# Opening of a convolution and SwiGLU kernel: how block 0's x is cut and loaded, when the first weights and block 1's x are issued, and one tap of the opening's plan

## The chip, the cores and the metric

The kernel runs on one core of one Trainium2 chip. The metric is the device time of one execution in microseconds (us). Three executions before the change took 771.68 (the median), 770.90 and 772.23 us. Times within the kernel are counted from the start of the profiled span.

The engines are named as in the profile: PE is TensorE's matmul, PEld its weight load, DVE is VectorE, ACT is ScalarE, POOL is GpSimd, SP is SyncE, which here only issues DMAs and passes semaphores on. A small q (SPq, POOLq) marks an engine's sequencer. Lines as L553 are lines of the kernel before the change.

## The reference: what is computed

A causal convolution of seven taps along the sequence, with softmaxed weights per head, and behind it a SwiGLU block. There are 8 sequences of 4096 tokens with 192 channels, 8 heads of 24 channels, and 1536 channels inside the second part.

```python
w = np.exp(weight - weight.max(-1, keepdims=True))
w = w / (w.sum(-1, keepdims=True) + 1e-09)                  # 8 heads x 7 taps
x_pad = concatenate([zeros((B, 6, D)), x], axis=1)          # causal
idx = arange(S)[:, None] + arange(7)[None, :]
out = einsum('hk,bskhg->bshg', w, x_pad[:, idx, :].reshape(B, S, 7, 8, 24))
x = out.reshape(32768, 192)
g = x @ w_gate
y = (g * (1 / (1 + exp(-g))) * (x @ w_val)) @ w_out         # 192 -> 1536 -> 192
```

## The kernel before

**Blocks and chunks.** The 32768 tokens are 64 blocks of 512, taken in 32 pairs. In a block the 1536 inner channels are 12 chunks of 128. For one chunk TensorE makes `gate` (L546) and `val` (L547) from the convolved x, three steps of 64 rows each, both at a time on the two halves of the array; ACT takes silu of the gate (L551), DVE multiplies it with val into `h` (L553), and TensorE multiplies h by `wo_sb` into `acc` (L558), one block behind. Chunks are counted through the whole kernel: 0 to 11 are block 0, 12 to 23 block 1, and so on. `late_start` gives the units of L558 in chunks 12 to 19: none in 12 and 13, six each from 14 on. After twelve units, at the end of chunk 15, the accumulation changes halves, and the next L558 has to wait for the last of the first half. That is done through `mark` (L440): a no-operation on SP that waits for the matmul, and for which the later matmul waits.

**Two ways to convolve.** From the second pair on, the convolution is done on channels by partitions: x is loaded in 32 x 32 squares (`emit_load`, L103, tiles sqA, sqB, and headA, headB for a sequence's first pair), transposed on DVE (`emit_turn`, L114, tiles xtA, xtB), and the seven taps are shared out by a plan: tap 0 on ACT into a PSUM bank, `run` (L473), further taps on ACT (L466), DVE (L483) or POOL (L488), and POOL adds the products and makes `xc` (L495, L501). The products of ACT and POOL cost one addition on POOL each, apart from the first; DVE's are added as they are made. SP then swaps the halves of xc (L449, L450) into `xs`. Each pair has three such groups. `plan_group` puts each step behind a chunk; `PLAN["opening"]` gives them for pair 1, as (turn, start, taps on ACT, taps on DVE, POOL, join, swap), one row for each group.

The first pair is convolved on TensorE, so that it can start without the transposed x. x is loaded token by token on partitions, in six overlapping pieces (windows) of a block, 85 tokens apart (`load_x`, tile x_sb, fp32; index 0 is block 0 and 1 is block 1). Block 0's pieces 3 to 5 go from ACT's queue, 1 and 2, then 0, and then all of block 1's from SP's. The band matrix of the taps, T, is built meanwhile: softmax on DVE and ACT (`wmax`, `soft`, `spun`, `left`), L310 (`repeat`) on TensorE, and four products with the 0/1 matrix `band` on DVE (L318, `cut_band`). The copy `flat` (L376) is one of their inputs. ACT and POOL cast block 0's pieces to fp16 (L229, tile x16); `heads` multiplies them by T (L334), two per head group, and `gather` (L392) puts channels into the order of the second part: D0, D1, D2, the operands of block 0's gate and val. Block 1's pieces are cast by POOL into x16p (L232, two casts, by parity of the head), and `lateA(0)`, `lateA(1)` and `lateC` convolve them in chunks 2, 5 and 8, with 48 matmuls of L334 each, into `foldA1` and `foldC1`, whose halves SP swaps for block 1 (L661).

**The orders around the change.** Each engine's instructions run in the order of the program. POOL: the four iotas (L171), `plain` and `mask` (L201 to L211), weights 0 to 3 (two DMAs, `load_w`, L158; they cast from fp32 to fp16), its cast of block 0's x, `spread` places 0 and 1, weights 4 to 7, places 2 and 3, `own`, the two casts of x16p, weights 8 to 11, `wo`, and then group 1's taps. SP: taps, block 0's x, block 1's x, the four headB loads of pair 1 (shown as sqB; they wait for the first `repeat`, L364), the first halves of headA (behind `lateA(0)`, L655), the swaps of foldA1 and foldC1, the second halves of headA (chunk 9), the swap of group 1 (chunk 13), and pair 2's loads from chunk 14 on.

PSUM: gates of block 0 rotate through two banks; those of chunks in `PLAN["third"]` (2 and 10) take the `run` bank instead, which group 1's tap 0 uses in between.

Of the kernel before, what the change touches and what calls it, by code (L numbers as in the profile page):

```python
# [15 lines left out]
    load=((2, -47), (3, -40), (0, -34), (1, -28)),  # L16
    opening=(
# [3 lines left out]
    ),  # L21
    gate=2, val=3, lead=4, third=(2, 10),
)


# [1 line left out]
def kernel(  # L27
# [9 lines left out]
    nc = tc.nc  # L37
# [16 lines left out]
    NCH = Dff // P  # L54
    pad = K - 1
# [3 lines left out]
    n_pairs = NT // (2 * TB)  # L59
    ppb = S // (2 * TB)  # L60
    x_flat = x.flatten_outer_dims()
# [14 lines left out]
    squares, xts = {}, {}  # L76
# [5 lines left out]
    def emit_load(q, part, half=None):  # L82
        head = q % ppb == 0
        if part == 2 and not half:
            squares[q, "A"] = headA if head else xpool.tile(
                [P, HIST + 2 * TB], fp32, tag="sqA", name="sqA"
            )
            squares[q, "B"] = headB if head else xpool.tile(
                [P, HIST + TB], fp32, tag="sqB", name="sqB"
            )  # L90
        for k in range(2):
            quad = 2 * (part % 2) + k
            if part < 2:
                tile_, t0, n, c = squares[q, "A"], 0, 2 * TB, SQ * quad
            else:
                tile_, t0, n, c = squares[q, "B"], TB * (part % 2), TB, P + SQ * k
            skip = HIST if head and t0 == 0 else 0
            row = q * 2 * TB + t0 - HIST + skip
            n = n // SQ + 1 - skip // SQ
            if half is not None:  # L100
                first = TB // SQ + 1
                skip, row, n = ((skip, row, first), (first * SQ, row + first * SQ, n - first))[half]
            nc.sync.dma_start(  # L103
                out=tile_[quad * SQ : (quad + 1) * SQ, skip : skip + n * SQ].rearrange("p (n c) -> p n c", c=SQ),
                in_=x_flat[row : row + n * SQ, c : c + SQ].rearrange("(n p) c -> p n c", p=SQ),
            )
# [9 lines left out]
    def sync_after(ins, earlier, why="one bank, two halves of the array"):  # L116
        tc.add_manual_dep(
            ins.ins,
            earlier.ins.name,
            mybir.DependencyInfo(mybir.DependencyClass.Sync, mybir.DependencyReason.DATA),  # L120
            reason=why,
        )

    HALF, STEP, W, NW = TB // 2, 85, 88, 6
    ROWS, LOADED = W + pad, 96
    ends = (0, STEP, 2 * STEP, HALF, 4 * STEP, 5 * STEP, TB)
    assert 8 == K + 1 and (NW - 1) * STEP + W > TB and HALF - 3 * STEP in (0, 1)
    RT = 8 * H  # L130
    taps = const_pool.tile([H, K], fp32, tag="taps", name="taps")
    nc.sync.dma_start(out=taps, in_=weight)
    x_sb = xpool.tile([P, 2, NW, D], fp32, tag="x_sb", name="x_sb", bufs=1)

    def load_x(b, lo, hi, skip=0, queue=nc.sync):
        queue.dma_start(
            out=x_sb[skip:LOADED, b, lo:hi, :],
            in_=bass.AP(
                tensor=x_flat.tensor,
                offset=x_flat.offset + (b * TB + lo * STEP - pad + skip) * D,  # L140
                ap=[[D, LOADED - skip], [STEP * D, hi - lo], [1, D]],
            ),
        )

    load_x(0, 3, NW, 0, nc.scalar)
    load_x(0, 1, 3)
    load_x(0, 0, 1, pad)
    load_x(1, 0, NW)
    w = wpool.tile([P, 3, Dff], fp16, tag="w_sb", name="w_sb")
    wo_r = wpool.tile([P, NCH, D], fp16, tag="wo_sb", name="wo_sb")  # L150
    w_halves = [
# [4 lines left out]
    def load_w(lo, hi, which):  # L156
        rows, src = w_halves[which]
        nc.gpsimd.dma_start(out=w[rows, :, lo * P : hi * P], in_=src[:, :, lo * P : hi * P])  # L158
# [4 lines left out]
    nc.vector.memset(one, 1.0)  # L163
    two = const_pool.tile([P, 1], fp32, tag="two", name="two")
    nc.scalar.activation(two, one, AF.Exp)
    nc.vector.memset(x_sb[0:pad, 0, 0, :], 0.0)


    def numbers(name, shape, pattern, base, dt=int32, step=1):
        t = const_pool.tile(shape, dt, tag=name, name=name)  # L170
        nc.gpsimd.iota(  # L171
            t, pattern=pattern, base=base, channel_multiplier=step, allow_small_or_imprecise_dtypes=True
        )
        return t
# [1 line left out]
    head = numbers("head", [H, H, 8], [[-1, H], [0, 8]], 0)  # L176
    far = numbers("far", [RT, 8, K], [[-1, 8], [1, K]], 8)
    row = numbers("row", [RT, RT], [[-1, RT]], 0)
    off = numbers("off", [P, W], [[-1, W]], 0)

    whose = const_pool.tile([H, H, 8], fp32, tag="whose", name="whose")
    rotate = const_pool.tile([RT, 8, K], fp32, tag="rotate", name="rotate")
# [3 lines left out]
    def where(out, t, bits):  # L186
# [11 lines left out]

    plain = const_pool.tile([P, 4, grp], fp16, tag="plain", name="plain")
    spread = const_pool.tile([P, 4, 2, DB], fp16, tag="spread", name="spread")  # L200
    nc.gpsimd.memset(plain, 0.0)  # L201
    nc.gpsimd.affine_select(
        out=plain, in_=plain, pattern=[[-32, 4], [-1, grp]],
# [8 lines left out]
        out=mask[:, :].rearrange("r (h c) -> r h c", h=H),  # L212
# [1 line left out]
        pattern=[[-8, H], [0, grp]],  # L214
        compare_op=ALU.not_equal, fill=1.0, base=0, channel_multiplier=1,
    )
    load_w(0, 4, 0)
    load_w(0, 4, 1)


    x16 = xpool.tile([P, NW, D + 8], fp16, tag="x16", name="x16", bufs=1)
    x16p = xpool.tile([P, 2, NW, D], fp16, tag="x16p", name="x16p", bufs=1)
# [5 lines left out]
    def cast(copy, lo, hi):  # L228
        copy(x16[0:ROWS, lo:hi, 0:D], x_sb[0:ROWS, 0, lo:hi, :])  # L229
# [7 lines left out]
    soft = const_pool.tile([RT, K + 1], fp32, tag="soft", name="soft")  # L237
# [20 lines left out]
    nc.scalar.activation(soft[:, 0:K], rows, AF.Exp, bias=wmax)  # L258
    where(band, off, 0)
    spun = const_pool.tile([RT, 8, K], fp32, tag="spun", name="spun")  # L260
    nc.vector.tensor_tensor(spun, rotate, soft[:, 0:K].unsqueeze(1).to_broadcast([RT, 8, K]), op=ALU.mult)
    turned = const_pool.tile([RT, 8], fp32, tag="turned", name="turned")
    nc.vector.tensor_reduce(wsum, soft, axis=AX.X, op=ALU.add)
    nc.vector.tensor_reduce(turned, spun, axis=AX.X, op=ALU.add)
# [6 lines left out]
    def repeated(t):  # L271
        return t[:, :].unsqueeze(1).to_broadcast([RT, REP, 8])
# [4 lines left out]
    nc.vector.tensor_tensor(full, turned, norm.to_broadcast([RT, 8]), op=ALU.mult)  # L277
    nc.vector.tensor_tensor(left[:, 1, :, :], repeated(full), left[:, 0, :, :], op=ALU.subtract)
    left = left[:, :, :, :].rearrange("r i n m -> r i (n m)")
    nc.scalar.activation(two, one, AF.Silu)  # L280
    cast(nc.scalar.copy, 0, 2)
    cast(nc.gpsimd.tensor_copy, 2, NW)

    def place(k):
        lo, hi, at = ((0, DB, 0), (DB, 96, 0), (0, 32, 32), (32, 96, 0))[k]
# [22 lines left out]
    def repeat(part, h0):  # L308
        bank = early[("hi", "lo")[part] + "AC"[h0 // HH]]
        return nc.tensor.matmul(  # L310
            bank[0:ROWS, 0 : HH * W], left[:, part, 0:ROWS],
            pick[:, h0 : h0 + HH, :].unsqueeze(2).to_broadcast([RT, HH, W // 8, 8]),
            start=True, stop=True,
        )
# [25 lines left out]
                        fresh.add((a, k))  # L340
        return ins

    def piece(win, t0):
        return ends[win] - win * STEP, slice(ends[win] - t0, ends[win + 1] - t0)

    def by_head(h):
        return [
            lambda e, w=w: (x16[0:ROWS, w, grp * h : grp * h + 32], h, *piece(w, 0))
            for w in (2, 3, 4, 5, 0, 1)
        ]  # L350

    def by_block(b, half):
        def of(e, w):
            h = 32 * b // grp
            h += (h + e) % 2
            return x16p[0:ROWS, e, w, 32 * b : 32 * b + 32], h, *piece(w, HALF * half)

        return [lambda e, w=w: of(e, w) for w in range(half * NW // 2, (half + 1) * NW // 2)]

    warm(3)  # L360
    warm(1, 2)
    some = repeat(0, 0)

    if n_pairs > 1:  # L364
        sync_after(nc.sync.nop(), some, "squares after x")
        for part in (2, 3):
            emit_load(1, part, None)
    repeat(1, 0)
    repeat(0, HH)
    repeat(1, HH)  # L370
# [17 lines left out]
    def heads(k, part):  # L388
        return convolve(sums[k], [by_head(HH * k + a) for a in range(4)], (part,), (0,))
# [318 lines left out]
    lead = PLAN["lead"]  # L708
# [4 lines left out]
    for n in range(2 * n_pairs):  # L713
        block = Block(n)
        for j in range(NCH):
# [6 lines left out]
            half = src.done // (2 * NCH) - 1 if units and src.done % (2 * NCH) == 0 else None  # L722
# [82 lines left out]
```

## Time and profile before

| what | us |
|---|---|
| median of three executions | 771.68 |
| the profiled execution | 770.74 |
| its span, first to last instruction | 769.0 |
| first gate matmul, L546 | 8.69 |
| first val matmul, L547 | 9.56 |
| first L334 on block 1's x (`lateA(0)`) | 11.60 |
| turn of group 1, xtB, on DVE | 15.03 |
| first L558 of block 0's second half | 26.46 |

Landing times of the opening's DMAs, from the trace (issue, landing; from each landing's last semaphore):

| DMA | issued by | issue | landed |
|---|---|---|---|
| block 0's x, pieces 3 to 5, 216 KB | ACT | 0.74 | 3.82 |
| block 0's x, pieces 1 and 2, 144 KB | SP | 1.21 | 4.33 |
| block 0's x, piece 0, 67.5 KB | SP | 1.61 | 5.58 |
| block 1's x, 432 KB | SP | 2.10 | 8.32 |
| weights 0 to 3, gate and val, 192 KB each | POOL | 2.69, 3.53 | 8.64, 9.51 |
| headB, four of 64 or 68 KB | SP | 4.82 to 6.25 | 9.89, 10.16, 11.35, 13.83 |
| weights 4 to 7 | POOL | 5.65, 6.28 | 11.50, 12.53 |
| weights 8 to 11 | POOL | 9.61, 10.24 | 14.23, 15.18 |
| wo, 576 KB | POOL | 10.86 | 19.86 |
| headA's first halves, the last three of four | SP | 12.71 to 14.20 | 19.69, 20.02, 20.65 |
| swap of foldA1, two | SP | 15.75, 18.19 | 20.84, 21.01 |
| swap of foldC1, two | SP | 19.08, 19.99 | 21.20, 21.89 |

How to read the lines below: a line of the chain of waits has start, length and what it was. A line of the timeline has start, length, engine, line, operation, out and in with shapes, how many were merged, and in brackets the engine's idle time before it and what ended that. A line of a DMA queue has its packets, MB, and the time that the packets took as a share of 16 engines' time; q1 is the queue of SP's DMAs, q0 of POOL's, q10 of ACT's. A packet of x_sb is 768 bytes, one of the weights 1 KB (as written), one of the squares 128 bytes.

### The profile page before, as it was taken

To read this page: it belongs to the slowest core of one execution; us is meant where nothing else is said; L and a number is where in the kernel's file an instruction comes from. 1 tells how busy PE (TensorE), PEld (TensorE's weight loads), DVE (VectorE), ACT (ScalarE), POOL (GpSimd) and SP (SyncE) were. 2 spreads that over 40 slices of the span, in tenths; PEclk is the share of its full clock that TensorE was granted. 3 is DMA by queue.
4 is the path that set the end of the run, shared out by engine and by line. 5 is a ranking of instruction groups with operands and counts; after the bars stand their busy time and mean duration, and the time that the engine had idled before them with its cause. 6 is when DMAs were issued, how large, how long until landed. Compare 5 with 4: busy or idle time off the path is not lost.

```text
span 769.0 us, 28288 instructions
## 1 busy us (share of the span) xinstructions
PE 762.0 (99%) x11035; PEld 585.2 (76%) x11035; DVE 658.8 (86%) x1051; ACT 660.4 (86%) x1187; POOL 668.7 (87%) x650
## 2 busy tenths in 40 slices
PE   8999999999999999999999999999999999999998
PEld 3777777777777777777777777777777777777776
DVE  7888988888888889888888888888888888888875
ACT  6888888888888888888888888888888888888875
POOL 6999998888998888988889988889888899888850
PEclk9999999999999999999999999999999999999999
DMA  9543343434344433434343344334444334443211
GB/s 169 107 88 89 81 88 83 100 81 88 85 90 86 91 85 82 90 87 93 85 86 90 85 88 90 90 78 89 92 89 88 84 88 86 89 94 87 60 47 53
DMA packets 255280, 67.27 MB, mean 87 GB/s; under 512 B 207919, under 2 KB 255145, under 8 KB 255145
## 3 DMA queue, kind: packets, MB, share of 16 engines
q1 hardware_dynamic: 252041, 63.47, 38.5%
q0 software_dynamic: 2800, 1.77, 1.7%
q8 instruction: 86, 1.41, 0.7%
q14 instruction: 49, 0.40, 0.2%
q10 hardware_dynamic: 304, 0.22, 0.1%
HBM read 29.64 MB, written 25.17 MB: 71 GB/s over the span
## 4 chain that ended last, share of the span: by engine, by line
PE 97%; DMA 1%; SPq 1%; POOL 0%; ACT 0%; issue 0%; DVE 0%; POOLq 0%; DVEq 0%; ACTq 0%
PE val L547 49%; PE acc L558 35%; PE gate L546 13%; DMA w_sb<-in_moe_w_val_dram 1%; SPq L103 1%; PE acc L756 0%; PE acc L334 0%; ACT silu L551 0%; PE val L756 0%; PE run L756 0%; POOL w_sb L158 0%; ACT run L473 0%; DVE xtB L114 0%; SPq L661 0%; SPq L450 0%
## 5 line engine op out<-in xcount | busy, mean ns | idle before, releaser
L553 DVE TENSOR_TENSOR h<-silu,val 128x512 f16<-128x512 f16 x768 | 509.3, 680 | 101.3 <-ACT silu L551 71.7
L551 ACT ACTIVATE silu<-gate 128x512 f16<-128x512 f32 x768 | 453.0, 594 | 79.3 <-PE gate L546 71.9
L558 PE MATMUL acc<-wo_sb,h 64*128 64x192 f16 x6048 | 470.2, 243 | 0.4 <-SPq L443 0.4
L495 POOL TENSOR_TENSOR t<-t,t 128x512 f32<-128x512 f32 x310 | 394.1, 1271 | 58.5 <-ACT t L466 36.6
L558 PEld LDWEIGHTS <-h 64*128 64x128 f16 x6048 | 395.2, 94 | 64.1 <-SPq L443 0.7
L547 PE MATMUL val<-xc,w_sb 64*128 64x512 f16 x1116 | 409.7, 376 | 0.0
L546 PE MATMUL gate<-xc,w_sb 64*128 64x512 f16 x1116 | 409.7, 376 | 0.0
L546 PE MATMUL gate<-xs,w_sb 64*128 64x512 f16 x1116 | 360.0, 376 | 0.0
L547 PE MATMUL val<-xs,w_sb 64*128 64x512 f16 x1116 | 360.0, 376 | 0.0
L547 PEld LDWEIGHTS <-w_sb 64*128 64x128 f16 x2340 | 212.0, 94 | 103.8 <-issue 2.0
L546 PEld LDWEIGHTS <-w_sb 64*128 64x128 f16 x2340 | 212.4, 94 | 5.6 <-issue 0.7
L501 POOL TENSOR_TENSOR xc<-t,aD 128x512 f16<-128x512 f32 x93 | 118.0, 1269 | 7.3
L488 POOL TENSOR_SCALAR t<-xtA,wn 128x512 f32<-128x512 f32 x155 | 106.1, 695 | 0.9 <-DVE xtA L114 0.9
L466 ACT ACTIVATE t<-xtA,wn 128x512 f32<-128x512 f32 x124 | 88.4, 713 | 0.0
L596 ACT COPY o<-acc 128x384 f32<-128x384 f32 x126 | 60.4, 479 | 19.7 <-DMA sqA<-in_x_dram 4.9
L488 POOL TENSOR_SCALAR t<-xtB,wn 128x512 f32<-128x512 f32 x63 | 42.9, 693 | 4.0 <-DVE xtB L114 4.0
L483 DVE SCALAR_TENSOR_TENSOR aD<-xtA,wn,run 128x512 f32<-128x512 f32 x62 | 46.0, 742 | 0.0
L466 ACT ACTIVATE t<-xtB,wn 128x512 f32<-128x512 f32 x61 | 43.6, 715 | 0.0
L473 ACT ACTIVATE run<-xtA,wn 128x512 f32<-128x512 f32 x62 | 42.5, 686 | 0.6 <-DVE xtA L114 0.6
L114 DVE STREAM_TRANSPOSE xtA<-sqA 128x544 f32<-128x544 f32 (+1 forms) x48 | 34.6, 722 | 0.0
L483 DVE SCALAR_TENSOR_TENSOR run<-xtA,wn,run 128x512 f32<-128x512 f32 x31 | 23.2, 750 | 0.0
L483 DVE SCALAR_TENSOR_TENSOR run<-xtB,wn,run 128x512 f32<-128x512 f32 x31 | 23.2, 750 | 0.0
(112 smaller groups left out, 178.1 us busy)
## 6 DMA issues: line engine op xcount, KB each, us to landing
out_dram<-o SPq DMA_DIRECT2D x127, 192.0 KB, 2.0
sqA<-in_x_dram SPq DMA_DIRECT2D x92, 132.0 KB, 2.8
xs<-xc SPq DMA_DIRECT2D x186, 64.0 KB, 2.0
sqB<-in_x_dram SPq DMA_DIRECT2D x96, 68.0 KB, 2.4
headA<-in_x_dram SPq DMA_DIRECT2D x28, 128.0 KB, 2.6
headB<-in_x_dram SPq DMA_DIRECT2D x14, 68.0 KB, 2.5
headB<-in_x_dram SPq DMA_DIRECT2D x14, 64.0 KB, 2.1
w_sb<-in_moe_w_gate_dram POOLq DMA_DIRECT2D x3, 192.0 KB, 5.9
```

What stands on the lines that cost most here:

```text
L466: mul(parts[-1], *self.tap(k))
L473: nc.scalar.mul(self.aD, *self.tap(0))
L483: nc.vector.scalar_tensor_tensor(out=self.aD, in0=v, scalar=s, in1=run, op0=ALU.mult, op1=ALU.add)
L488: self.product(k, lambda t, v, s: nc.gpsimd.tensor_scalar(t, v, scalar1=s, scalar2=1.0, op0=ALU.mult, op1=ALU.mult), self.parts)
L495: nc.gpsimd.tensor_tensor(self.parts[0], self.parts[0], t, op=ALU.add)
L501: nc.gpsimd.tensor_tensor(xc, self.parts[0], self.aD, op=ALU.add)
L546: nc.tensor.matmul(g, w[0:DB, ca, f], a[0:DB, :], start=(i == 0), stop=(i == 2))
L547: nc.tensor.matmul(v, w[DB:P, cb, f], b[DB:P, :], start=(i == 0), stop=(i == 2))
L551: nc.scalar.activation(s, self.g.pop(j), AF.Silu)
L553: nc.vector.tensor_tensor(h, s, self.v.pop(j), op=ALU.mult)
L558: ins = nc.tensor.matmul(acc, self.h[j][r, ts(s, P)], wo_r[r, j, :], start=first and j == 0, stop=not first and j == NCH - 1, skip_group_c ...
L596: nc.scalar.copy(self.o[:, 2 * half : 2 * half + 2, :], self.acc[:, :, 0:D])
```

## The change

Five things are changed, all in the opening.

- Block 0's pieces begin at token 0, and not six tokens ahead of it, so that no rows have to be zeroed: `starts` has a row for block 0 and one for block 1. The pieces of both come as 96 rows, block 0's in two DMAs (pieces 3 to 5 from ACT, 0 to 2 from SP). `band`, T and the products are 96 columns wide and not 88; ROWS stays 94. `off` starts at 8, which shifts the band.
- ACT casts three pieces of block 0 and POOL three, before two and four.
- Weights 0 to 3 are issued on POOL right behind the iotas, ahead of `plain` and `mask`.
- Block 1's x is issued in two DMAs behind a no-operation on SP that waits for `spun`, and the headB loads of pair 1 follow right behind them, before behind the first `repeat`.
- In the opening's plan for group 1 one tap goes from DVE to ACT, the join moves from chunk 8 to 9 and the swap from 13 to 14; chunk 10's gate no longer takes the `run` bank.

```diff
-        (4, 5, (7,), (6, 7), 7, 8, 13),
+        (4, 5, (7, 9), (6,), 7, 9, 14),
...
-    gate=2, val=3, lead=4, third=(2, 10),
+    gate=2, val=3, lead=4, third=(2,),
...
-    HALF, STEP, W, NW = TB // 2, 85, 88, 6
-    ROWS, LOADED = W + pad, 96
-    ends = (0, STEP, 2 * STEP, HALF, 4 * STEP, 5 * STEP, TB)
+    HALF, STEP, W, NW = TB // 2, 85, 96, 6
+    ROWS, LOADED = 94, 96
+    starts = (
+        (0, STEP, 2 * STEP, HALF - pad, HALF - pad + STEP, HALF - pad + 2 * STEP),
+        tuple(STEP * i - pad for i in range(NW)),
+    )
+    ends = (
+        (0, STEP + pad, 2 * STEP + pad, HALF, HALF + STEP, HALF + 2 * STEP, TB),
+        (0, STEP, 2 * STEP, HALF, 4 * STEP, 5 * STEP, TB),
+    )
+
+    column = lambda b, win, t: t - starts[b][win] - pad + 8
...
-    def load_x(b, lo, hi, skip=0, queue=nc.sync):
+    def load_x(b, lo, hi, queue=nc.sync):
         queue.dma_start(
-            out=x_sb[skip:LOADED, b, lo:hi, :],
+            out=x_sb[0:LOADED, b, lo:hi, :],
...
-                offset=x_flat.offset + (b * TB + lo * STEP - pad + skip) * D,
-                ap=[[D, LOADED - skip], [STEP * D, hi - lo], [1, D]],
+                offset=x_flat.offset + (b * TB + starts[b][lo]) * D,
+                ap=[[D, LOADED], [STEP * D, hi - lo], [1, D]],
...
-    load_x(0, 3, NW, 0, nc.scalar)
-    load_x(0, 1, 3)
-    load_x(0, 0, 1, pad)
-    load_x(1, 0, NW)
+    load_x(0, 3, NW, nc.scalar)
+    load_x(0, 0, 3)
...
-    nc.vector.memset(x_sb[0:pad, 0, 0, :], 0.0)
...
-    off = numbers("off", [P, W], [[-1, W]], 0)
+    off = numbers("off", [P, W], [[-1, W]], 8)
...
+    load_w(0, 4, 0)
+    load_w(0, 4, 1)
     nc.gpsimd.memset(plain, 0.0)
...
-    load_w(0, 4, 0)
-    load_w(0, 4, 1)
...
+    sync_after(nc.sync.nop(), spinning, "block 1's x behind the first weights")
+    load_x(1, 0, 3)
+    load_x(1, 3, NW)
+    if n_pairs > 1:
+        for part in (2, 3):
+            emit_load(1, part, None)
     nc.scalar.activation(two, one, AF.Silu)
-    cast(nc.scalar.copy, 0, 2)
-    cast(nc.gpsimd.tensor_copy, 2, NW)
+    cast(nc.scalar.copy, 0, 3)
+    cast(nc.gpsimd.tensor_copy, 3, NW)
...
-            for w in (2, 3, 4, 5, 0, 1)
+            for w in (3, 4, 5, 0, 1, 2)
...
-    some = repeat(0, 0)
-
-    if n_pairs > 1:
-        sync_after(nc.sync.nop(), some, "squares after x")
-        for part in (2, 3):
-            emit_load(1, part, None)
+    repeat(0, 0)
```

`spinning` is the name now given to the product `spun` on DVE. `piece` takes the block as an argument, and finds its first column by `column`.

More of the change, by code (lines that the diff above doesn't have):

```diff
@@ L122, in sync_after @@
         )
-    HALF, STEP, W, NW = TB // 2, 85, 88, 6
-    ROWS, LOADED = W + pad, 96
-    ends = (0, STEP, 2 * STEP, HALF, 4 * STEP, 5 * STEP, TB)
-    assert 8 == K + 1 and (NW - 1) * STEP + W > TB and HALF - 3 * STEP in (0, 1)
+    HALF, STEP, W, NW = TB // 2, 85, 96, 6
[9 more added lines that the diff above has]
+    column = lambda b, win, t: t - starts[b][win] - pad + 8
+    assert 8 == K + 1 and all(
+        2 <= column(b, i, ends[b][i]) and column(b, i, ends[b][i + 1]) <= ROWS - pad + 8
+        for b in range(2) for i in range(NW)
+    )
     RT = 8 * H
@@ L260 @@
     spun = const_pool.tile([RT, 8, K], fp32, tag="spun", name="spun")
-    nc.vector.tensor_tensor(spun, rotate, soft[:, 0:K].unsqueeze(1).to_broadcast([RT, 8, K]), op=ALU.mult)
+    spinning = nc.vector.tensor_tensor(spun, rotate, soft[:, 0:K].unsqueeze(1).to_broadcast([RT, 8, K]), op=ALU.mult)
     turned = const_pool.tile([RT, 8], fp32, tag="turned", name="turned")
@@ L341, in convolve, with piece @@
         return ins
-    def piece(win, t0):
-        return ends[win] - win * STEP, slice(ends[win] - t0, ends[win + 1] - t0)
+    def piece(b, win, t0):
+        return column(b, win, ends[b][win]), slice(ends[b][win] - t0, ends[b][win + 1] - t0)
     def by_head(h):
         return [
-            lambda e, w=w: (x16[0:ROWS, w, grp * h : grp * h + 32], h, *piece(w, 0))
-            for w in (2, 3, 4, 5, 0, 1)
+            lambda e, w=w: (x16[0:ROWS, w, grp * h : grp * h + 32], h, *piece(0, w, 0))
+            for w in (3, 4, 5, 0, 1, 2)
         ]
@@ L355, in of @@
             h += (h + e) % 2
-            return x16p[0:ROWS, e, w, 32 * b : 32 * b + 32], h, *piece(w, HALF * half)
+            return x16p[0:ROWS, e, w, 32 * b : 32 * b + 32], h, *piece(1, w, HALF * half)
         return [lambda e, w=w: of(e, w) for w in range(half * NW // 2, (half + 1) * NW // 2)]
```

## The prediction

> **What bounds the kernel now.** I read the page's chain first: its shares say that from end to end the time is TensorE's.
>
> ```profile
> PE 97%; DMA 1%; SPq 1%; POOL 0%; ACT 0%; issue 0%; DVE 0%; POOLq 0%; DVEq 0%; ACTq 0%
> ```
>
> Then the busy time by stretch. Columns are the stretch, its length, and the busy time of PE, weight load, DVE, ACT and POOL, the clock, the DMA share and GB/s. TensorE idles 17.86 - 15.63 = 2.23 us between its first weights and 26.46, and 0.03 us in the next 33 us.
>
> ```profile
> 8.60:26.46 17.86, 15.63 (x303) 9.24 (x304) 14.53 (x28) 13.18 (x24) 12.87 (x15) 1.00 0.99 142
> 26.46:60.00 33.54, 33.51 (x525) 25.75 (x527) 28.94 (x47) 29.02 (x53) 31.67 (x33) 1.00 0.50 102
> ```
>
> So this change can act only by moving the moment at 26.46 from which TensorE never waits again; every microsecond there is one at the end. The chain of the first 40 us, in order of time (start, length, what), says what sets that moment.
>
> ```profile
> 2.73 0.80 POOL w_sb L158
> 3.53 5.98 DMA w_sb<-in_moe_w_val_dram
> 9.56 0.39 PE val L547
> ...
> 11.67 0.58 PE acc L334 x48
> ...
> 15.11 0.66 DVE xtB L114
> ...
> 23.95 0.47 SPq L449
> 24.46 0.59 SPq L450
> 25.10 0.58 SPq L103
> 25.73 0.52 SPq L103
> 26.46 1.17 PE acc L558 x24
> ```
>
> The first weights (landed 9.51) start TensorE. At the other end stands SP's queue: TensorE's second half of an accumulation (L558) waits for two no-operations on SP (`mark`, L443), and these are queued behind the swap of group 1 (L449, L450) and two loads (L103). The swap needs `xc` of group 1, which POOL makes from `xtB`. POOL's timeline shows both ends of that.
>
> ```profile
> 8.38 1.28 POOL L232 CAST x16p<-x_sb 94x576 f16<-94x576 f32 x2 [0.77 <-DMA x_sb<-in_x_dram]
> ...
> 15.87 1.38 POOL L488 TENSOR_SCALAR t<-xtB,wn 128x512 f32<-128x512 f32 x2 [3.95 <-DVE xtB L114]
> 17.33 1.28 POOL L495 TENSOR_TENSOR t<-t,t 128x512 f32<-128x512 f32 x1
> ...
> 22.06 1.27 POOL L501 TENSOR_TENSOR xc<-t,aD 128x512 f16<-128x512 f32 x1
> ```
>
> POOL starts 0.11 after `xtB` (15.03 + 0.73 = 15.76) and gives `xc` at 23.33, 7.46 later. SP reached the swap only at 23.91 (its own loads came first), so POOL had 0.58 to spare. From 23.91 to TensorE's start at 26.46 SP needs 2.55.
>
> The last view is what the DMA queues did in three stretches of 0.75 us: 4.25 to 5.00, where q1 (SP's) carries block 1's x alone; 5.75 to 6.50, where q0 (POOL's weights) has joined; 12.25 to 13.00, where q0 has weights 8 to 11 and q1 has just been given sqA.
>
> ```profile
> q1 hardware_dynamic: 255, 0.19, 97.6%
> ```
> ```profile
> q0 software_dynamic: 77, 0.08, 81.9%
> q1 hardware_dynamic: 73, 0.05, 44.7%
> ```
> ```profile
> q0 software_dynamic: 151, 0.14, 116.5%
> q1 hardware_dynamic: 17, 0.00, 3.3%
> ```
>
> Alone, x moves 255 / 0.75 = 340 packets per us; beside weights each queue moves about 100.
>
> **Weights first (moved).** The issues leave 2.69 for the end of the iotas, 1.55, and the four operations they pass (1.55 to 2.69, 1.13 us) end later instead, at about 4.18. POOL's cast of x started at 4.46 after x landed at 4.33, so these are hidden, and 576 columns for 768 end it near 4.85 instead of 5.28. q0's first packet came 2.5 us after the issue (5.19); now 4.1.
>
> **Block 0's x (two transfers, no zeros).** A 0.22 memset and one SP issue (0.45) go. Pieces 0 to 2 land as one 288-packet transfer; the nearest rows are ACT's of the same 216 KB, 3.1 us after issue, and the old first piece, 4.0: 4.3 to 5.2. ACT's cast grows from 384 to 576 columns, 0.51 to about 0.68 (by 0.51 for 384 and 0.82 on POOL for 768, nearer its own), and starts near 4.8, not 5.67. But DVE's four band products hold the rest: they start at 4.83 both times and grow by 384/352 (three steps of 0.435 to 0.475, +0.12), against 0.35 of waiting for `flat` that goes (the L310 matmuls ahead of them, 0.31 each, grow by 0.03). D1 and D2 come about 0.2 earlier: 8.9 and 9.0. If the transfer lands at 5.6, ACT's `flat` is late and the 0.2 is gone.
>
> **First matmuls.** Before, nine pairs (0.215 each) ran from 9.56 to 11.5. If weights land by 8.9, two pairs go ahead of D1 and seven follow: 10.42, 1.08 earlier. This is the most that the start can give.
>
> **Block 1's x (held).** Its issue moves from 2.10 to behind `spun` (ends 3.50): two issues at 3.55 and 3.95, then sqB's four at 4.4 instead of 4.82. It is 96 x 6 = 576 packets, the first 1.4 after the issue (as 1.21 to 2.57 before), at 4.9. Before, it had the engines nearly to itself until 5.2 and landed at 8.32. Now weights 0 to 3 (384 packets, some 60 gone by 4.9) stand beside it from its first packet: at 100 per us they end near 8.1 with 320 of x moved, and weights 4 to 7 (issued near 5.3, packets 2.5 later) follow without a hole, so x ends at 10.7 and lands 0.8 to 1.4 later. That is the high bound, 12.1. The low one is the old 6.2 from issue to landing: 3.55 + 6.2 = 9.8, or 9.2 if only the old 3.0 us of packets and 1.3 of landing count. I take **11.0**, nearer to the row with both queues at work.
>
> [...]
>
> **What is queued behind x.** POOL's two casts of x16p (0.66 each) wait for both transfers; behind them on POOL stand weights 8 to 11 and wo. Landing L gives the casts' end at L + 1.34. The 48 matmuls of `lateA(0)` need the second cast for their last three quarters (0.44) and end at L + 1.9: 12.9, against 12.25. From there to the end of `xtB` were 15.76 - 12.25 = 3.51: two chunks, silu, the h products, `wn`, all unchanged. So `xtB` ends at L + 5.4 = 16.4 (sqB, now behind a later x, landed last at 13.83 and has 1.2 to spare). Weights 8 to 11 move from 9.61 to 12.4, land 4.6 and 4.9 after their issues, 17.0 and 17.9, where chunk 8 wants them at 17.12 + 0.65 = 17.8; wo lands at 13.6 + 9.0 = 22.6 for a use at 23.9.
>
> **The opening's plan.** One tap of group 1 moves from DVE (0.75) to ACT (0.72), which puts one more POOL addition (1.27, with the step 1.30) into `xc`: 8.87 from the end of `xtB`, not 7.57. The swap at chunk 14 instead of 13 passes nothing on SP. Chunk 10's gate leaves the `run` bank, which takes away a wait of 0.48; that wait lies ahead of 26.46 and under SP's, so it gives nothing unless SP is early.
>
> **Sum.** `xtB` + 8.87 + 2.55 is TensorE's start: L + 5.4 + 11.42 = L + 16.82, against 26.46. The change in time is L - 9.6, with a floor of -0.36 where the start itself is the limit (`xtB` at 15.76 - 1.08 = 14.68). With L = 11.0: 9.51 -> 9.0 for the weights, but **+1.4 us**. On the profiled execution, 770.74 (769.0 span and 1.7 around it), that is 772.1; on the median, 0.9 above it, 771.68 + 1.4 = **773.1**. About 0.2%, 1.5 us, is what a measurement of this kernel tells from no change, so the forecast lies at that line.
>
> **Rivals.** (a) x lands early, 9.8 or before: the weights leave gaps that x fills. For it: x's last contended packets started at 6.96, only 1.8 after weights began. Against: then weights had just begun, and were 28 packets by 5.75. -0.36 to +0.2: 771.6. (b) SP is the limit by itself. The stretch at 12.25 shows q1 at 17 packets while q0 runs; SP's issue of swapA then took 2.4, until 18.15. wo is issued 13.6 - 10.86 = 2.7 later, so if that stall is the weights' doing it ends at 20.85; swapA's second 0.6, swapC 1.6, four loads 3.3, then 2.55: 28.9, +2.4, 774.1. It decides once the stall lasts beyond 19.8 (19.8 + 8.0 is 27.9). Against: q0 now has a hole before weights 8, in which sqA can move. (c) **Faster**: TensorE's own path decides. It was ready for L558 at 25.9; less 1.08, 0.48 for the bank and 0.34 for swapC's landing it is 24.0, -2.4, 769.3, if POOL's `xc` is there by 21.5. That needs x by 9.3 and `xtB` at 12.6, or additions far below 1.27; for it, every wait named in the opening lies before the part that moves; against, no row has such an addition. (d) That the change doesn't do what it says, weights not landing sooner, changes nothing: TensorE waits for x16p anyway; it counts with the forecast.
>
> **How the numbers follow.** Forecast 0.50, (a) 0.19, (b) 0.18, (c) 0.13. The forecast's own range is L from 10.3 to 12.1, +0.7 to +2.5: 772.4 to 774.2, half of it above 1.5. Slower by over 0.2%: 0.25 + 0.18 = 0.43; within: 0.25 + 0.19 = 0.44; faster: (c), 0.13. The range over all is 770.9, below (a), to 774.9, above (b), and leaves out (c) and the end of (b).
>
> **What would show it.** Weights issued on POOL at 1.55 and landed by 9.1; x16p's casts starting near 11.0 with POOL idle before them, and TensorE idle before the first L334 on x16p (0.5 us or more, where it now starts at 11.60 without a DMA wait); `xtB` ending near 16.4; `xc` 8.9 after it; SP's L449 starting as `xc` ends, not after loads; the first run of 24 L558 near 27.9. I am wrong if the casts start before 9.8, if L449 starts later than `xc` by over 0.3, or if the 24 start before 26.

## The result and the profile after

| | before | after |
|---|---|---|
| median of 13 executions, us | 771.41 (770.16 to 772.23) | 772.98 (771.28 to 774.08) |
| the profiled execution, us | 770.74 | 774.08 |
| its span, us | 769.0 | 772.3 |

The ratio of the times is 1.0020, with an interval of 1.0011 to 1.0028: the change makes the kernel 1.6 us slower. The profiled execution after is the longest of its 13, so its marks lie later than those of a typical one; a second profile of the same kernel (`after_again`, below) has a span of 770.3 and is the second shortest of its ten. Times and marks are read from both.

The shares of the page's chain after the change, from end to end, are still TensorE's:

```profile
PE 97%; POOL 1%; DMA 1%; DVE 0%; SPq 0%; issue 0%; ACT 0%; POOLq 0%; DVEq 0%
```

The same two stretches as before, with the same columns (stretch, length, busy time of PE, weight load, DVE, ACT and POOL, clock, DMA share, GB/s):

```profile
8.60:26.46 17.86, 16.93 (x286) 8.72 (x288) 13.22 (x26) 12.37 (x23) 11.74 (x13) 1.00 0.92 125
26.46:60.00 33.54, 31.82 (x509) 24.40 (x505) 27.59 (x44) 28.33 (x52) 31.64 (x34) 1.00 0.50 98
```

In the first, TensorE is busy for 16.93 us where it was 15.63, with fewer matmuls (286 for 303). So it isn't waiting more there, its matmuls take longer. In the second it stands idle for 1.72 us (0.03 before), 1.36 of them ahead of the 24 L570 (L558 before), whose start is now at 29.19. From there to the end of the span it is 743.1 us, 742.5 before: 2.7 of this execution's 3.3 us were lost by then.

The chain of the first 30 us after (start, length, what; lines have moved by some ten: L284 was L274, L327 was L310, L351 was L334, L404 was L392, L558 was L546, L500 was L488, L513 was L501, L461 was L449, L570 was L558):

```profile
3.95 1.00 DVE left L284
4.99 0.55 PE hiA L327
...
8.57 1.82 PE D L404 x4
10.39 0.54 PE gate L558
...
13.65 0.58 PE acc L351 x48
...
17.09 0.66 DVE xtB L114
...
17.84 1.38 POOL t L500 x2
...
25.37 1.28 POOL xc L513
26.67 0.47 SPq L461
...
29.19 1.17 PE acc L570 x24
```

Two things differ from the chain of before. The weights' DMA no longer stands at its head: DVE's `left` does, with 1.00 us, and behind it TensorE's own matmuls, one after the other. And POOL's additions are in it, from `xtB` to `xc`, with SP's swap starting 0.02 us after `xc` ends, where it started 0.6 after before. A DMA of block 1's x is in neither chain.

What became of `left` and of its neighbours is seen in the timeline of DVE, POOL and TensorE after (start, length, engine, line; in brackets the idle time before and what ended it). The rows of `left` and of POOL's cast in the profile before stand in a fence of their own.

```profile
3.95 0.99 DVE L284 TENSOR_TENSOR left<-turned,norm 64x96 f16<-64x96 f32 x1
...
4.17 0.66 POOL L239 CAST x<-x_sb 94x576 f16<-94x576 f32 x1
...
4.99 0.55 PE L327 MATMUL hiA<-pick,left 64*94 64x384 f16 x1 [0.62 <-DVE left L284]
```

```profile
3.84 0.25 DVE L274 TENSOR_TENSOR left<-turned,norm 64x96 f16<-64x96 f32 x1
...
4.46 0.82 POOL L229 CAST x<-x_sb 94x768 f16<-94x768 f32 x1 [0.29 <-DMA x_sb<-in_x_dram]
```

The same operation on as many elements takes 0.99 us instead of 0.25, and ends 0.11 after POOL's cast rather than before the cast begins. The cast begins at 4.17, not 4.46. What POOL has to do ahead of it ends at about the same time in both (the issue of the weights at 4.17 before, the select for `mask` at 4.22 after). But before, POOL then waited 0.29 for pieces 1 and 2 of x, which landed at 4.33; now its three pieces are all of ACT's transfer, which landed at 3.67, and it waits for nothing. DVE's chain is a little later (3.95, not 3.84). TensorE stands idle for 0.62 us and begins L327 at 4.99, not 4.30.

### The profile page after: what moved, and what is told of

The parts are those of the page before. It is cut to its first block, busy times and chain, and to the rows that moved or that the text cites. A ratio compares the mean times of both kernels' runs of the same rounds, so it can differ in the third digit from the quotient of the medians.

```text
span 772.3 us, 28288 instructions
## 1 busy us (share of the span) xinstructions
PE 765.1 (99%) x11035; PEld 613.4 (79%) x11035; DVE 659.4 (85%) x1049; ACT 662.2 (86%) x1188; POOL 668.7 (87%) x651
## 4 chain that ended last, share of the span: by engine, by line
PE 97%; POOL 1%; DMA 1%; DVE 0%; SPq 0%; issue 0%; ACT 0%; POOLq 0%; DVEq 0%
PE val L559 39%; PE acc L570 31%; PE gate L558 25%; POOL t L507 1%; DMA xs<-xc 1%; PE acc L768 0%; POOL t L500 0%; PE D L404 0%; PE idle L259 0%; POOL xc L513 0%; SPq L103 0%; PE val L768 0%; DVE left L284 0%; PE run L768 0%; PE hiA L351 0%
## 5 line engine op out<-in xcount | busy, mean ns | idle before, releaser
L570 PE MATMUL acc<-wo_sb,h 64*128 64x192 f16 x6048 | 436.0, 243 | 1.3 <-SPq L455 1.2
L570 PEld LDWEIGHTS <-h 64*128 64x128 f16 x6048 | 377.0, 94 | 62.9 <-SPq L455 2.2
L558 PE MATMUL gate<-xc,w_sb 64*128 64x512 f16 x1116 | 409.8, 376 | 0.0
L558 PE MATMUL gate<-xs,w_sb 64*128 64x512 f16 x1116 | 360.3, 376 | 0.0
L558 PEld LDWEIGHTS <-w_sb 64*128 64x128 f16 x2340 | 212.6, 94 | 27.5 <-issue 3.4
L513 POOL TENSOR_TENSOR xc<-t,aD 128x512 f16<-128x512 f32 x93 | 118.1, 1270 | 7.3
L500 POOL TENSOR_SCALAR t<-xtA,wn 128x512 f32<-128x512 f32 x155 | 105.8, 693 | 0.4 <-DVE xtA L114 0.4
L500 POOL TENSOR_SCALAR t<-xtB,wn 128x512 f32<-128x512 f32 x63 | 42.9, 693 | 4.8 <-DVE xtB L114 4.8
L495 DVE SCALAR_TENSOR_TENSOR aD<-xtB,wn,run 128x512 f32<-128x512 f32 x31 | 23.0, 742 | 0.0
```

The source lines that it names most:

```text
L495: nc.vector.scalar_tensor_tensor(out=self.aD, in0=v, scalar=s, in1=run, op0=ALU.mult, op1=ALU.add)
L500: self.product(k, lambda t, v, s: nc.gpsimd.tensor_scalar(t, v, scalar1=s, scalar2=1.0, op0=ALU.mult, op1=ALU.mult), self.parts)
L513: nc.gpsimd.tensor_tensor(xc, self.parts[0], self.aD, op=ALU.add)
L558: nc.tensor.matmul(g, w[0:DB, ca, f], a[0:DB, :], start=(i == 0), stop=(i == 2))
L570: ins = nc.tensor.matmul(acc, self.h[j][r, ts(s, P)], wo_r[r, j, :], start=first and j == 0, stop=not first and j == NCH - 1, skip_group_c ...
```

## The experiments

Two theories were to be told apart from the one on record (x late) and from its rivals. **Collision**: the earlier cast of POOL holds up DVE's `left`, and with it the band products and TensorE. **Pace**: TensorE runs at half its pace for the first microseconds, and the moment at which it goes to full pace decides how early `xtB` comes. Beside them stands the part of the prediction that wasn't in doubt, the **plan** (one more addition on POOL, and the later swap).

How the pace is read: in these shapes (512 columns) successive pairs of gate and val start 0.427 us apart at first and 0.215 apart later. "Full pace from" below is the moment from which it is 0.215, read to some 0.1 to 0.4 where matmuls of other shapes or a gap lie in between. E is the start of the first run of 24 L570 (L558 in kernels made from the one before).

| kernel | median, us | ratio to before, interval | first `left` takes | full pace from | last D ready | `xtB` ends | E | E less `xtB` |
|---|---|---|---|---|---|---|---|---|
| before (profile shown above) | 771.41 | 1 | 0.25 | 4.63 | 9.22 | 15.77 | 26.46 | 10.69 |
| before_again | 771.04 | 0.9997, 0.9988 to 1.0006 | 0.25 | 9.41 | 10.12 | 16.08 | 26.41 | 10.33 |
| before_third | 770.94 | 0.9997, 0.9988 to 1.0006 | 0.25 | about 10.1 | 9.99 | 15.96 | 26.38 | 10.42 |
| after | 772.98 | 1.0020, 1.0011 to 1.0028 | 0.99 | 12.80 | 11.02 | 17.74 | 29.19 | 11.45 |
| after_again | 773.12 | 1.0023, 1.0014 to 1.0033 | 0.99 | 10.30 | 11.02 | 16.54 | 27.96 | 11.42 |
| cast_held | 771.90 | 1.0010, 1.0001 to 1.0019 | 0.35 | 9.46 | 10.19 | 15.73 | 27.16 | 11.43 |
| warm_more | 772.05 | 1.0011, 1.0001 to 1.0020 | 0.98 | 4.79 | 9.53 | 15.26 | 26.70 | 11.44 |
| old_plan | 772.30 | 1.0015, 1.0005 to 1.0025 | 0.98 | 10.46 | 11.02 | 16.58 | 28.19 | 11.61 |
| held_warm | 771.99 | 1.0014, 1.0005 to 1.0023 | 0.35 | 9.48 | 10.38 | 16.04 | 27.48 | 11.44 |
| held_warm_plan | 771.55 | 1.0003, 0.9994 to 1.0012 | 0.35 | before 4.8 | 9.13 | 16.34 | 26.67 | 10.33 |
| weights_late | 772.86 | 1.0021, 1.0012 to 1.0030 | 0.25 | 9.84 | 10.66 | 16.24 | 27.68 | 11.44 |
| x_free | 772.85 | 1.0021, 1.0012 to 1.0030 | 0.98 | 9.56 | 10.66 | 16.39 | 27.82 | 11.43 |
| before_plan | 772.26 | 1.0011, 1.0002 to 1.0020 | 0.25 | 12.40 | 11.12 | 17.59 | 29.02 | 11.43 |
| before_fill | 771.51 | 1.0003, 0.9994 to 1.0012 | 0.25 | 9.05 | 10.38 | 16.14 | 26.87 | 10.73 |

Medians are of ten or eleven executions (13 in the first comparison). They stand in three groups, each compared with the executions of before made beside it (medians 771.09, 771.25 and 771.14 over some 30): after_again to old_plan, held_warm to x_free, and the rest. A profile is one execution: those of after_again, warm_more and weights_late are 0.9 to 1.0 shorter than their medians, those of after and before_plan 1.1 and 2.0 longer. In weights_late and before_plan POOL's cast meets `full` and not `left`; `full` then takes 0.86 and 0.78, and 0.15 when it is alone.

**The changed kernel once more** (after_again, no edit).

> The changed kernel once more, for a second profile. Theory S (start): DVE's first product left (0.99 in the changed kernel, 0.25 before) waits out POOL's cast of x, which now begins at 4.17; TensorE idles from 4.37 to 4.99 and its matmuls keep half the pace (0.43 from start to start for 512 columns) until 12.6. S expects left near 1.0 again, the idle again, and half pace for some 5 to 8 us again; the first run of 24 L570 at 28 to 29.5. If the pace is a matter of the single execution, the end of the half pace moves by some us and the time with it; left stays. Theory X (the forecast): block 1's x lands at 10.9 or later and TensorE stands before the first L351 on x16p. In the first profile it landed at 9.43; X needs it later here. Theory P (plan): the one more addition on POOL makes the loss; xc ends 8.9 after xtB in every run of this plan.

The ratio repeats. The profile doesn't: the same program, with the same landing of x (9.45, against 9.43), has E 1.23 us earlier, and up to the end of D2 (11.02 both times) the two are alike. What differs is the moment of full pace, 10.30 instead of 12.80: half of those 2.5 us is the 1.2 by which `xtB` is earlier.

**POOL's cast held back until DVE's two `left` are done** (cast_held):

```diff
-        copy(x16[0:ROWS, lo:hi, 0:D], x_sb[0:ROWS, 0, lo:hi, :])
+        return copy(x16[0:ROWS, lo:hi, 0:D], x_sb[0:ROWS, 0, lo:hi, :])
...
-    nc.vector.tensor_tensor(left[:, 1, :, :], repeated(full), left[:, 0, :, :], op=ALU.subtract)
+    lefts = nc.vector.tensor_tensor(left[:, 1, :, :], repeated(full), left[:, 0, :, :], op=ALU.subtract)
...
-    cast(nc.gpsimd.tensor_copy, 3, NW)
+    sync_after(cast(nc.gpsimd.tensor_copy, 3, NW), lefts, "pool's cast behind left")
```

> The changed kernel with POOL's cast of block 0's x held until DVE's second left has ended (POOL starts it near 4.5 instead of 4.17). S: left back to 0.25, first L327 at 4.3 as before the change, full pace (0.215) by the first gate matmul at about 9, lateA(0) from 10.9, xtB ending near 15, the 24 L570 near 26.4; time 1.5 to 2.5 us under the changed kernel, within 0.5 of the kernel before. X: x lands no earlier, so no gain over 0.5 us. P: no gain.

Its timeline of DVE and POOL:

```profile
3.95 0.35 DVE L284 TENSOR_TENSOR left<-turned,norm 64x96 f16<-64x96 f32 x1
...
4.41 0.25 DVE L288 TENSOR_TENSOR left<-full,left 64x96 f16<-64x96 f32 x1
```

```profile
4.72 0.66 POOL L239 CAST x<-x_sb 94x576 f16<-94x576 f32 x1 [0.51 <-DVE left L288]
```

`left` starts at the same 3.95 as after and takes 0.35 instead of 0.99. POOL's cast comes 0.55 later, and the kernel is still better for it: the medians lie 1.2 us apart, the two ratios 0.0013, E 0.80. The collision is real and worth most of a microsecond: six of the ten executions of after_again are longer than the longest of cast_held (772.67). The intervals of the two ratios overlap, so the size is no closer known than that. The 0.10 that remains of `left`, and 0.11 of `spun` (0.32 here and after, 0.21 before and in weights_late), fall beside POOL's selects, which the weights have passed.

**Five warming matmuls ahead of L327 instead of three** (warm_more), which fill the 0.62 us that TensorE stood idle, and leave the collision in:

```diff
-    warm(3)
+    warm(5)
     warm(1, 2)
```

> The changed kernel with five warming matmuls in place of three ahead of L327, so that TensorE works until 5.2 and has no idle time before left; left keeps its wait for POOL's cast. S, if the idle time is what costs the pace: L327 starts at 5.25 and full pace comes at about 5 to 6; the first gate matmul near 9.5, lateA(0) near 11.5; time 1 to 1.5 us under the changed kernel. S, if the late left alone is what costs: half pace as before and no gain, 0.2 us lost. X and P: no gain.

In its profile, the shortest of its ten (771.10), `left` still takes 0.98 and L327 still begins at 5.00, but full pace begins at 4.79 and the last D is ready at 9.53, 1.5 us earlier than after. The median falls by 1.1. Whether the two more matmuls made the pace, or this execution had it by chance, one profile can't say: before had 4.63 in one and 9.4 or more in two, and of the two kernels below with a fourth warming matmul one has it and one not.

**The plan and the `third` of before in the changed kernel** (old_plan):

```diff
-        (4, 5, (7, 9), (6,), 7, 9, 14),
+        (4, 5, (7,), (6, 7), 7, 8, 13),
...
-    gate=2, val=3, lead=4, third=(2,),
+    gate=2, val=3, lead=4, third=(2, 10),
```

> The changed kernel with the plan of the kernel before (one tap less on ACT, one more on DVE, swap at chunk 13, chunk 10's gate in the run bank). P: xc ends 7.6 after xtB, the 24 L570 start 1.3 earlier than in the changed kernel, or as early as SP's own loads allow, 0.8 earlier; time 0.8 to 1.3 us under the changed kernel. S: the start of the kernel is unchanged (xtB at 17.0 if the pace is as slow), the same 0.8 to 1.3 for the plan's part, as the two are in series. X alone: under 0.3 us.

`xc` now ends at 24.13, 7.55 after `xtB`, as before; but E comes only at 28.19. SP's queue shows why:

```profile
17.15 3.87 SPq L673 DMA_DIRECT2D swapA<-foldA  x2
...
22.34 3.24 SPq L103 DMA_DIRECT2D sqA<-in_x_dram  x4
25.68 0.47 SPq L461 DMA_DIRECT2D xs<-xc  x1
```

Its two issues of swapA take 3.87 (3.23 of it the first), and SP reaches the swap 1.5 us after `xc` is ready. This is rival (b)'s stall; with the new plan it is hidden behind POOL's longer additions (in after the two issues take 3.46, and SP is free 0.9 before `xc` is ready).

**cast_held with four warming matmuls** (held_warm: the edit of cast_held, and `warm(4)` for `warm(3)`), and **the same with the plan and the `third` of before** (held_warm_plan: those two edits too).

> The changed kernel with POOL's cast held behind DVE's second left and four warming matmuls in place of three. In the five profiles so far the moment from which TensorE never waits (the first run of 24 L570) is the end of xtB + 11.42 to within 0.03, as in the prediction, for the new plan; what differs is xtB, and that follows the end of TensorE's half pace (4.6 before, 4.8 with five warming matmuls, 9.5 to 12.8 elsewhere). Theory C (the clock): without an idle time and with one more warming matmul the full pace comes near 5; L327 at 4.7, the first gate matmul at 8.3 to 8.6, lateA(0) at about 10.9, held by block 1's x (landing 9.4, casts to 10.8); xtB ends near 15.0, the 24 at 26.4: time within 0.5 us of the kernel before. Theory S (left alone): as the run with only the cast held, +0.8 over before.

> The same with the plan of the kernel before. xc 7.6 after xtB, at about 22.6. C and P: POOL no longer sets the swap; SP's own loads do, which end at 23.9 before the change and would end some 0.6 earlier if lateA(0) does: the 24 at 25.6 to 26.0, time 0.3 to 0.9 us under the kernel before. If SP's swap of foldA1 stalls as in the run with the old plan (3.2 us at 17.15), the 24 come at 26.5 or later and nothing is won.

Filling the idle time brought nothing beyond the hold (1.0014 against 1.0010, each within the other's interval), and full pace came at 9.48 all the same: it isn't got by filling this gap alone. Without the new plan, the time is that of before as far as can be measured, 1.0003. Its profiled execution had full pace before 4.8 and the last D at 9.13, and lost that again to weights 4 to 7, which landed late (13.57 for val); `xtB` ended at 16.34 and E was 26.67.

**The first weights issued where they were before** (weights_late: the two `load_w(0, 4, ...)` back behind `mask`).

> The changed kernel with weights 0 to 3 back behind plain and mask; the rest of the change stays. Theory S/C: POOL is busy issuing from 2.69 to 4.17 as before the change, its cast starts at 4.2 again beside left, or after left has begun at 3.84: if left began first it keeps 0.25 and TensorE has no idle time; full pace at 4.6 to 5. Weights land at 8.6 and 9.5 and hold the first matmuls at 9.5. The 24 at about 27, from the plan's 1.3 less SP's 0.6: +0.5 to +0.9 over the kernel before. Theory X: x without the weights beside it lands earlier than 9.4.

This gains nothing over after (1.0021), and it shows the collision at another instruction. DVE and POOL:

```profile
3.84 0.25 DVE L284 TENSOR_TENSOR left<-turned,norm 64x96 f16<-64x96 f32 x1
4.02 0.86 DVE L287 TENSOR_TENSOR full<-turned,norm 64x8 f32<-64x8 f32 x1
4.91 0.29 DVE L288 TENSOR_TENSOR left<-full,left 64x96 f16<-64x96 f32 x1
```

```profile
4.17 0.68 POOL L239 CAST x<-x_sb 94x576 f16<-94x576 f32 x1
```

`left` is through at 0.25 this time, and `full`, a twelfth of its size, takes 0.86 in its stead. The second `left` begins only at 4.91, against 5.14 after and 4.41 in cast_held. So the price follows the cast of POOL, not the place of the weights: the cast begins at 4.17 with either. What lets it begin there is its new share of the pieces, which needs ACT's transfer alone; that is read from the traces, since no run gives POOL its old share back in the changed kernel.

**Block 1's x issued right behind block 0's** (x_free), the no-operation that waits for `spinning` kept ahead of the headB loads:

```diff
     load_x(0, 0, 3)
+    load_x(1, 0, 3)
+    load_x(1, 3, NW)
...
-    sync_after(nc.sync.nop(), spinning, "block 1's x behind the first weights")
-    load_x(1, 0, 3)
-    load_x(1, 3, NW)
     if n_pairs > 1:
+        sync_after(nc.sync.nop(), spinning, "squares after x")
```

> The changed kernel with block 1's x issued right behind block 0's (1.6, 2.0), the headB loads behind spun. Theory X (the forecast's step): x lands near 8.0 instead of 9.4, and the weights later than 7.6; if x had been the limit the time falls by over 1 us. Theories S and C: left's wait and the half pace are unchanged, x is not waited for in either kernel, so the 24 stay at 28 to 29 and the time within 0.4 us of the changed kernel.

The tile's own view of x16p, first of after and then of x_free (engine, operation, count, shortest, median and longest duration in ns, first and last start):

```profile
L242 POOL CAST x16p<-x_sb x2: 657/658/660, 9.6 to 10.2; 94x576 f16<-94x576 f32 x2
```

```profile
L244 POOL CAST x16p<-x_sb x2: 657/660/662, 10.5 to 11.2; 94x576 f16<-94x576 f32 x2
```

Issued 2 us earlier, x landed 1 us later (10.41, against 9.43 and 9.45), and the weights too (9.81, against 7.61 and 7.50). The time stayed: 1.0021. TensorE's weight loads waited 0.4 us for x16p there, its matmuls not; in after neither waited. What the queues moved from 5 to 6 us, first in after and then in x_free (q0 has the weights, q1 block 1's x):

```profile
q0 software_dynamic: 173, 0.16, 104.6%
q1 hardware_dynamic: 18, 0.01, 9.8%
```

```profile
q0 software_dynamic: 104, 0.10, 62.8%
q1 hardware_dynamic: 176, 0.13, 49.9%
```

In after the weights go first and x follows (298 packets from 6 to 7, beside 58 of the weights). In x_free the two move side by side (134 beside 123 from 6 to 7).

**Before again, twice** (before_again, before_third, no edit), to see what the pace of before's first profile was worth.

> The kernel before, for a second profile. In the profiles so far TensorE's full pace begins at 4.6 (the kernel before), 4.8, and otherwise at 9.5 to 12.8, among these in two kernels whose left was on time and whose TensorE had no idle time before 5.9. [...] Theory S: the kernel before has 4.6 each time, and the 24 at 26.4 to 26.6.

> The kernel before, for a third profile; as above. [...]

Full pace began at 9.41 and about 10.1, not at 4.63. The spreading matmuls and the first gate of before_again:

```profile
7.61 1.03 PE L392 MATMUL D<-foldA,spread 128*128 128x512 f16 x2
...
9.43 0.39 PE L546 MATMUL gate<-D,w_sb 64*128 64x512 f16 x1
```

and of the profile that the prediction was made from:

```profile
7.41 0.59 PE L392 MATMUL D<-foldA,spread 128*128 128x512 f16 x2
```

The same pair takes 1.03 us in one execution and 0.59 in the other. E is 26.46, 26.41 and 26.38 in the three: in the kernel before, this is hidden, since SP's own queue sets E.

**The plan and the `third` of the changed kernel in the one before** (before_plan, the edit of old_plan turned round).

> The kernel before with the plan of the changed kernel alone. Theory P (the plan's one more addition on POOL, as in the prediction): xc ends 8.87 after xtB, and the first run of 24 L558 starts at the end of xtB + 11.42; with SP's spare time of 0.58 in the first profile that is 0.7 over the kernel before: +0.5 to +1.0 us. If the plan costs nothing: within 0.3 us, and the loss lies in the start alone.

1.0011: the plan alone costs, with the opening as it was before. The profiled execution is again the longest of its kernel (774.28 beside a median of 772.26). In it the taps landed late, so that `left` started at 4.39 and POOL's cast, from 4.50, held up `full`; full pace began at 12.40, and with E less `xtB` at 11.43 all of that arrived at the end. So the opening of the kernel before can have the collision too; in its own three profiles the cast began at 4.27 to 4.46, when the first `left` and `full` were done.

**Two more full-width matmuls behind the four L310 of the kernel before** (before_fill: `warm(2)` after `repeat(1, HH)`).

> The kernel before with two more warming matmuls behind the four of L310, where TensorE waits for the casts anyway. [...] S: the kernel before has its full pace at 4.6 anyway; no gain, or 0.1 to 0.2 us lost to the matmuls.

Full pace began at 9.05, not at the 4.6 that S took for granted, and the time is that of before or 0.4 above it (1.0003). The two matmuls more did not bring an early full pace in this execution. What exactly brings it stays open.

## Why the prediction came out as it did

The size was foretold (+1.4, measured +1.6); the mechanism was half right. That the size came out is in part luck: 0.6 of the 1.4 is the late landing of x (`xtB` at 16.4, not 15.76), which played no part, and a loss of about that size that the forecast didn't have, 0.8, stands in its place.

**Held: the plan and SP's queue.** The formula was E = end of `xtB` + 8.87 + 2.55 = + 11.42. In the eight profiles with the new plan it is 11.42 to 11.45. `xc` ends 8.90 after `xtB` (8.88 in after_again; 8.87 was forecast), and L461 starts as `xc` ends. The plan alone, put into the kernel before, costs 1.1 us.

**Failed: the landing of block 1's x, L = 11.0, and with it `xtB` = L + 5.4.** x landed at 9.43 (9.45), the casts started at 9.56, before the 9.8 named as the mark of being wrong, and no matmul waited for them: the 48 of `lateA(0)` started at 13.58 and 12.37, 2.7 and 1.5 after the casts' end. Rival (a)'s condition was met, and its time (771.6) was not, because the landing decided nothing. The forecast had weights and x move side by side at 100 packets per us each. In the trace the weights' first packet came at 3.13, not 4.1, and from 5 to 6 us they moved 173 packets beside 18 of x (shown above); they were in by 7.61, and x had the engines mostly to itself from 6 to 8 (0.21 and 0.27 MB in the two microseconds on its queue, with the first squares behind it, beside 0.05 and 0.01 on the weights'). x_free is the direct test: landing 1 us later still, the same time.

**Failed: "these are hidden", of the four operations that the weights pass, and "they start at 4.83 both times", of the band products.** This is what stands in the place of L. The forecast had the time of POOL's cast about right (an end near 4.85, measured 4.83) and counted its earlier end as a gain; it didn't ask who else is held while the cast runs. `left` takes 0.99 beside it, the band products start at 5.58, TensorE's L327 0.69 later than before, and the D tiles end 0.9 later than in before_again (10.70 and 11.02, against 9.80 and 10.12; forecast 8.9 and 9.0, from a profile at full pace). The traces show that these small products of DVE take longer beside the cast (`left` 0.99 and `full` 0.86, 0.25 and 0.15 without it), and that which of the two starts first didn't decide it. In before_plan `full` started behind the cast (4.57 and 4.50) and took 0.78; in weights_late it started ahead of it by the trace (4.02 and 4.17) and took 0.86. `left` in after started at 3.95, when POOL's select was under way (3.83 to 4.22), which may be what held it first. Why DVE and POOL are in each other's way here isn't shown by any run.

**Not seen: TensorE's pace.** The prediction took 0.215 for a pair from a profile in which the full pace began at 4.63. In eleven of the thirteen other profiles it began between 9.05 and 12.80; in the two others, warm_more and held_warm_plan, before 5. The kernel before bears this because SP has its own reason to start at 23.9. With the new plan E follows `xtB`, and so the pace: E goes from 26.70 (full pace from 4.79) over 27.16 (9.46) and 27.96 (10.30) to 29.02 and 29.19 (12.40 and 12.80). These are different kernels in part; the two of the same program are 27.96 and 29.19.

**The sum.** after_again, cast_held and before_again can be compared, because their pace is alike where it counts: half until the last matmul of D, full from the first gate. E is 27.96, 27.16 and 26.41. The 0.80 between the first two is the collision: the last D is ready 0.83 later and `xtB` 0.81. The 0.75 between the other two is the plan, less what hid it: 1.35 for the addition (8.89 from `xtB` to `xc`, not 7.54), less 0.25 that SP had to spare, less 0.35 by which `xtB` came later in before_again, where TensorE waited 0.26 for weights 4 to 7. Together they are 1.55. That the medians of the first comparison differ by 1.57 is in part luck, since these are single executions, and the first profile after has E at 29.19. The medians of the runs put the two parts at 1.2 and 0.8, and the four combinations agree with a price for each: collision and new plan 1.0020 and 1.0023, new plan without collision 1.0010 and 1.0014, collision with the old plan 1.0015, neither 1.0003. Each of these is known to 0.0009 or 0.0010 only, and old_plan shows that the parts don't simply add, since SP's stall is then bared.

**The rivals.** (b) decided only where the plan was put back. (c) had it that TensorE's own path decides, and in part it did, with the opposite sign, since that path had become longer, not shorter (`xtB` at 16.54 and 17.74, where (c) needed 12.6). (d) did not occur: the weights landed 1.9 us sooner, and it was worth nothing, since TensorE then waited for its own D. Even before the change the first weights held TensorE in only one of the three profiles of that kernel: in before_again and before_third it waited for none of them (landed at 9.23 and 9.32).

**Open.** No kernel tried was faster than before. What sets the moment of full pace, and why one or two warming matmuls more don't bring it reliably, wasn't settled. The two-transfer load of block 0's x was not undone by itself; its transfers landed at 3.67 and 4.30, at or before the early end of the forecast.

## What to carry to other kernels

When a step is cut anew, look at the wait that it loses: here POOL's cast no longer waited for a transfer, began 0.10 to 0.29 us earlier, and ran into another engine's short operations. The saving that was sought (weights 1.9 us sooner) was real and useless. A resource that looks slack in one profile may be the cover for something that varies from one execution to the next: take a second profile of the kernel before pricing what the cover hides. And price a moved step by who is held while it runs, not only by when it ends.

## What the runs showed of the hardware

**TensorE's half pace.** Matmuls of 512 columns start 0.427 us apart for the first 9 to 13 us of eleven of the fourteen profiles (0.215 later), although TensorE had been at work from 1.0 us on; in the three others the full pace began before 5. The clock column of the stretches doesn't show it: before_again has 1.00 in a stretch that is at half pace up to its end.

```profile
1.00:9.40 8.40, 8.40 (x113) 3.76 (x113) 5.29 (x25) 5.64 (x10) 7.93 (x21) 1.00 0.99 185
```

It shows in the busy time of the stretch from 8.60: 16.93 us for 286 matmuls after, with half pace until 12.80, where the first profile of before has 15.63 for 303. The moment varies between executions of one program: 4.63, 9.41 and about 10.1 in three of before, 12.80 and 10.30 in two of after. How long TensorE had been at work doesn't give it either: in the line above TensorE is busy for all of 8.40 us and still at half pace, and in the first profile of before it was busy for all of 3.63 us, from 1.00 to 4.63, when the full pace began. What sets the moment isn't shown by any run here.

**Small vector operations beside a cast.** A DVE product of 64 x 8 took 0.86 us (weights_late) and one of 64 x 96 0.99 (after), against 0.15 and 0.35 when the cast of POOL (0.66) was held back (cast_held).

**Transfers issued together.** Block 1's x issued at 1.61 and 2.11, together with the weights, landed at 10.41, and issued at 3.63 and 3.99, behind them, at 9.43. The weights landed at 9.81 and 7.61. Issued together, the two queues moved 123 and 134 packets from 6 to 7 us; issued apart, 58 and 298. Why x, issued earlier, ends later isn't settled by that.
